# Causal attention and a gated MoE layer on one core: several 32-column blocks in one VectorE transpose, the 1e-9 added on ScalarE or GpSimd, and a table of offsets for the planner's due times

## The chip, the core and the metric

The kernel runs on one core of a Trainium2 chip. The metric is the device time of one execution in microseconds (us), the median of several runs.

The engines are named as the profile names them: PE is TensorE (PEld its weight loads), DVE is VectorE, ACT is ScalarE, POOL is GpSimd, and SP is SyncE, which here issues nearly all DMAs.

## The reference

```python
# q, k, v: (4, 12, 448, 64); w_gate, w_val: (768, 1536); w_out: (1536, 768), all float32
scores = scale * np.matmul(q, k.transpose(0, 1, 3, 2))
mask = np.triu(np.ones((seq, seq), dtype=bool), k=1)
scores = np.where(mask, -1000000000.0, scores)
scores = scores - np.max(scores, axis=-1, keepdims=True)
attn = np.exp(scores)
attn = attn / (np.sum(attn, axis=-1, keepdims=True) + 1e-09)
attn_out = np.matmul(attn, v).astype(np.float32)
x = np.ascontiguousarray(attn_out.transpose(0, 2, 1, 3)).reshape(B * S, H * D)   # (1792, 768)
g = x @ w_gate
silu = g * (1.0 / (1.0 + np.exp(-g)))
out = (silu * (x @ w_val) @ w_out).astype(np.float32)
```

## The kernel before, in words

**Chunks and units.** The work is cut into four chunks, one for each batch element (448 tokens). The attention of a chunk has 12 heads, numbered as units: units 0 to 11 are chunk 0, 12 to 23 chunk 1, 24 to 35 chunk 2, 36 to 47 chunk 3. Two heads make a pair that shares its loads. While the MoE products of one chunk run on PE, the attention of the next chunk is computed beside them. In the names of tiles the first number is the unit or the chunk: `S46_0_0` holds scores of unit 46, `M2_4` is the fifth gate or value product of chunk 2 (even numbers gate, odd ones value), `MO1_3` the fourth block of outputs of chunk 1. Chunks 2 and 3 share their products in a Strassen-like scheme (`early`, `pair`, `outputs`; tiles `Bb` and `Be`).

**Precision.** PE multiplies float32 as three products of a high and a low part (`xh`, `xl`, and the two halves of `whl`), lines 1063 to 1065. So each weight tile of 128x768 has to be split before PE can use it: a copy for the high part (L338, L341, L344), a subtraction for the low part (L360 on DVE, L363 on POOL). PSUM has two banks for the products, tag `M`, and `whl` has four buffers.

**One unit of attention** (`attention`, L437). Scores on PE (L555); the mask and the row maximum in one DVE instruction with a small read of the accumulator behind it (L606); the exponential on ACT with the row sums as a by-product (L618); the reciprocal of the sums on DVE (`recip`, L626); the division, on ACT, POOL or DVE (L663, L667, L671); a transposition; and the product with V (`weigh`). The sums of a unit lie in a tile of 128x4, one column for each block of rows.

**The 1e-9.** `recip` adds it by a reduction over two slots of `all_sums`, that of the unit and one that holds 1e-9, and takes the reciprocal of the result:

```python
sm, rc = all_sums[:, u % NR :: NR - u % NR, i0:i1], rec[u % NR][:, i0:i1]
nc.vector.tensor_reduce(rc, sm.rearrange("p a c -> p c a"), mybir.AxisListType.X, ALU.add)
nc.vector.reciprocal(rc, rc)
```

**The transposition.** For chunk 0 and five of the six pairs of chunk 1, PE transposes 128x128 blocks into PSUM (L730, L735, L770). For one pair of chunk 1 and all of chunks 2 and 3 it goes another way (`turn`, L789): DVE transposes 32x32 blocks within SBUF (L818), DMAs write the result to DRAM in another order (L838 to L841) and read it back. Each DVE instruction handles 128 columns of one block of rows. An even unit takes 1, 2 and 3 of them for its row blocks 1 to 3, an odd one 1, 2, 3 and 4 for its row blocks 0 to 3:

```python
for t in range(i, 2 * i + 1) if odd else range(i):
    ...
    nc.vector.transpose(s["stage"][:r, :, at : at + G],
                        s[f"pp{i}"][:r, P * t : P * t + P].rearrange("p (c n) -> p c n", c=4))
```

**The order of the work.** Nothing is scheduled on the chip. While the program is built, a planner (`Planner.run`, L109) keeps a modelled clock for each engine and picks, of the operations that could start next on an engine, the one with the earliest due time; where several engines can do an operation it also picks the engine. Due times come from constants: `LEN` and `ATT` say where a stage lies, `SLOPE`, `BOOST`, `WLEAD` and others how far an operation is due ahead of its use. What comes out is one fixed list for each engine, and each engine works its list strictly in order: an instruction that waits holds up everything behind it on that engine.

**What the gate does** (`activate`, L1091). When a gate product is done, ACT takes its tanh (L1097) and DVE multiplies it in (L1100); only then is its bank of PSUM free for a later product. When the value product is done, DVE multiplies again (`finish_h`, L1114).

## Time and profile before

| | |
|---|---|
| median of 3 runs | 642.06 us (640.26 to 642.89) |
| the profiled execution | 640.58 us, its span 638.8 us |
| PE busy | 624.3 us, 98% of the span, 3590 matmuls |
| DVE busy | 528.3 us, 83%, 1289 instructions |
| ACT busy | 406.0 us, 64%, 966 instructions |
| POOL busy | 247.2 us, 39%, 293 instructions |
| mean granted clock of PE | 0.997 of full speed |

The span runs from the first to the last instruction, and 1.8 us of the time lie around it. The ends of matmuls are modelled, and one begins before the last has ended, so a busy PE says that matmuls were under way, and not that they followed each other at their fastest; idle time of PE is certain. A wait is put down to the releaser that came last by the profile.

### The profile page before, as it was taken

The page shows a single profiled execution, that of the slowest core. Times are in us where ns is not written, and L with a number is a line of the kernel's source. Part 1 is how long each engine was busy: PE and PEld are TensorE (multiplying, and loading weights), DVE is VectorE, ACT ScalarE, POOL GpSimd, SP SyncE. Part 2 cuts the span into 40 slices and gives each one's busy share as a digit, 9 for nine tenths or more (in the row PEclk, how much of TensorE's full clock was granted, in tenths as well). Part 3 has the DMA queues.
Part 4 walks back from the last instruction along what each step waited for, and adds up shares of the span by engine and source line. Part 5 has one row for each costly group of instructions (what it writes and reads, how often), then busy time and mean ns, then how long its engine had stood idle before and what let it go on. Part 6 is the DMA issues. An engine that isn't in the chain of part 4 may idle for free.

```text
span 638.8 us, 11236 instructions
## 1 busy us (share of the span) xinstructions
PE 624.3 (98%) x3590; PEld 561.7 (88%) x3590; DVE 528.3 (83%) x1289; ACT 406.0 (64%) x966; POOL 247.2 (39%) x293
## 2 busy tenths in 40 slices
PE   9999999999999999999999988799999999999997
PEld 6569989899999999999999977699999999999997
DVE  6989889898899788979799999889998889895320
ACT  6999668597785557657768987865554444471100
POOL 3754623355263345444434555442024244440000
PEclk9999999999999999999999999899999999999999
DMA  8869987998877668683878678787353331156311
GB/s 279 292 221 309 285 301 263 351 330 297 290 283 227 238 184 268 202 257 96 264 237 261 204 213 265 234 294 243 117 160 128 127 105 62 77 168 196 107 44 43
DMA packets 72668, 136.08 MB, mean 213 GB/s; under 512 B 18081, under 2 KB 45473, under 8 KB 72609
## 3 DMA queue, kind: packets, MB, share of 16 engines
q1 hardware_dynamic: 72304, 135.04, 64.5%
q8 instruction: 28, 0.46, 0.3%
q10 hardware_dynamic: 304, 0.33, 0.2%
q14 instruction: 32, 0.25, 0.1%
HBM read 98.34 MB, written 37.00 MB: 212 GB/s over the span
## 4 chain that ended last, share of the span: by engine, by line
PE 83%; DVE 8%; DMA 4%; ACT 3%; issue 1%; SPq 0%; ACTq 0%; DVEq 0%
PE M L1063 10%; PE M L1064 9%; PE M L1065 9%; PE MO L1063 8%; PE MO L1064 8%; PE MO L1065 8%; PE S L555 5%; PE O L932 4%; PE Bb L1375 3%; PE Bb L1377 3%; PE Bb L1376 3%; PE T L770 2%; DMA wide<-in_w_dram 2%; PE Be L1375 2%; PE Be L1376 2%; PE Be L1377 2%
## 5 line engine op out<-in xcount | busy, mean ns | idle before, releaser
L1063 PE MATMUL M<-xh,whl 128*128 128x448 f32 x360 | 134.2, 373 | 6.8 <-DVE t(2, 2, 't')_5663 L1100 3.6
L1065 PE MATMUL M<-xh,whl 128*128 128x448 f32 x360 | 131.0, 364 | 0.9 <-DVE whl L360 0.9
L1064 PE MATMUL M<-xl,whl 128*128 128x448 f32 x360 | 130.9, 364 | 0.0
L360 DVE TENSOR_TENSOR whl<-wraw,whl 128x768 fp32r<-128x768 f32 x89 | 89.4, 1013 | 12.7 <-ACT whl L338 12.2
L618 ACT ACTIVATE p<-p,m 128x192 f32<-128x192 f32 (+3 forms) x180 | 91.2, 509 | 6.8 <-DVE m L606 6.3
L338 ACT ACTIVATE whl<-wraw 128x768 fp32r<-128x768 f32 x65 | 54.5, 840 | 40.8 <-PE MO L1065 23.5
L1063 PEld LDWEIGHTS M<-xh,whl 128*128 128x128 f32 x360 | 67.9, 189 | 13.4 <-DVE t(2, 2, 't')_5663 L1100 3.9
L606 DVE CUSTOM_DVE_ANT_0 p<-S,masks 128x192 f32<-128x192 f32 (+3 forms) x180 | 69.1, 426 | 8.2 <-PE S L555 7.9
L1065 PEld LDWEIGHTS M<-xh,whl 128*128 128x128 f32 x360 | 67.9, 189 | 6.1 <-DVE whl L360 1.3
L1064 PEld LDWEIGHTS M<-xl,whl 128*128 128x128 f32 x360 | 68.0, 189 | 3.8
L1063 PE MATMUL MO<-h,whl 128*128 128x448 f32 x162 | 59.4, 367 | 0.0
L1064 PE MATMUL MO<-h,whl 128*128 128x448 f32 x162 | 58.7, 362 | 0.0
L1065 PE MATMUL MO<-h,whl 128*128 128x448 f32 x162 | 58.5, 361 | 0.0
L663 ACT ACTIVATE p<-p,rec 128x320 f32<-128x320 f32 (+3 forms) x123 | 52.5, 482 | 4.5 <-DVE rec L631 4.1
L818 DVE STREAM_TRANSPOSE w<-p 128x128 f32<-128x128 f32 x192 | 40.6, 272 | 0.5 <-ACT p L663 0.2
L1049 DVE SCALAR_TENSOR_TENSOR wraw<-wide,top 128x768 uint32<-128x768 uint32 x36 | 35.9, 996 | 5.8 <-ACT top L338 4.7
L555 PEld LDWEIGHTS S<-KS,QS 64*128 64x128 f32 (+1 forms) x432 | 29.5, 174 | 6.6 <-issue 4.6
L618 ACT ACTIVATION_READ_ACCUMULATOR p<-p,m 128x1 f32 (+1 forms) x180 | 34.0, 189 | 0.0
L1063 PE MATMUL MO<-last,whl 128*128 128x448 f32 x90 | 33.4, 371 | 0.0
L555 PE MATMUL S<-KS,QS 64*128 64x448 f32 (+3 forms) x432 | 32.5, 295 | 0.4 <-POOL KS L363 0.4
L1064 PE MATMUL MO<-last,whl 128*128 128x448 f32 x90 | 32.6, 362 | 0.0
L1065 PE MATMUL MO<-last,whl 128*128 128x448 f32 x90 | 32.5, 361 | 0.0
(380 smaller groups left out, 1518.1 us busy)
## 6 DMA issues: line engine op xcount, KB each, us to landing
wide<-in_w_dram SPq DMA_DIRECT2D x36, 768.0 KB, 7.2
wraw<-wr SPq DMA_DIRECT2D x66, 384.0 KB, 4.3
wr<-wraw SPq DMA_DIRECT2D x36, 384.0 KB, 4.2
wr<-wr SPq DMA_DIRECT2D x24, 384.0 KB, 4.2
x<-dO SPq DMA_DIRECT2D x12, 608.0 KB, 6.1
vraw<-in_v_dram SPq DMA_DIRECT2D x24, 256.0 KB, 3.9
qraw<-in_q_dram SPq DMA_DIRECT2D x23, 224.0 KB, 4.9
kraw<-in_k_dram SPq DMA_DIRECT2D x23, 224.0 KB, 5.4
```

The lines of the kernel that those rows point to most:

```text
L338: nc.scalar.activation(out(), in_(), AF.Copy, scale=scale)
L360: r["DVE"] = (cost("DVE", "two", n), lambda: nc.vector.tensor_tensor(out(), a(), b(), alu))
L555: nc.tensor.matmul(st[u + y][f"S{i}"][:r], Q[:, q0 : q0 + r], K[:, :q1_] if y else K[:, S - q1_ :], start=z == 0, stop=z == len(passes) - 1)
L606: nc.vector.tensor_tensor_reduce(p[:r], s[f"S{i}"][:r], mask[:r, maskX - q0 : maskX - q0 + q1_] if h % 2 else back[:r, P - min(q1_, P) : P ...
L618: nc.scalar.activation(p[:r], p[:r], AF.Exp, bias=peak(i)[:r], scale=-1.0, accum_out=sums[u % NR][:r, i : i + 1],)
L663: nc.scalar.activation(p[:r], p[:r], AF.Copy, scale=rec[u % NR][:r, i : i + 1])
L818: nc.vector.transpose(s["stage"][:r, :, at : at + G], s[f"pp{i}"][:r, P * t : P * t + P].rearrange("p (c n) -> p c n", c=4))
L1049: nc.vector.scalar_tensor_tensor(w["raw"].bitcast(U32), z, 13, top, ALU.logical_shift_right, ALU.bitwise_or)
L1063: nc.tensor.matmul(out[:, :n], a[:, w], xhi, start=first, stop=False, skip_group_check=True)
L1064: nc.tensor.matmul(out[:, :n], a[:, w], xlo, start=False, stop=False, skip_group_check=True)
L1065: nc.tensor.matmul(out[:, :n], l[:, w], xhi, start=False, stop=bool(last), skip_group_check=True)
L1375: nc.tensor.matmul(ps[key][:, :T], sh, hi, start=first, stop=False, skip_group_check=True)
```

## The change

Three things are changed together.

1. `turn` looks for runs of 128-column blocks whose places in the staging tile are evenly spaced, and transposes such a run by one DVE instruction with a four-dimensional access pattern. So that runs occur, the even units keep their two groups of blocks in the other order in the staging tile, and the readers (`view`, `groups`) take them from there. The planner's price of it goes from 0.06 us and 128 columns for each block to 128 columns for each block and 0.138 us for each instruction.
2. The reduction leaves `recip`. The 1e-9 is added to the unit's sums in place, either by ACT or by POOL, as the planner chooses; `recip` then waits for this addition.
3. The planner's constants are others, and every due time gets an offset from a table, `SHIFT`, by the name of the function that made the operation and its numbers. The table has 332 entries, from -96.43 to 58.75.

```diff
-SLOPE0 = 1.25
-WLEAD = 1.54
-XD = [-10.0, 3.0]
+SLOPE0 = 1.515
+WLEAD = 1.415
+XD = [6.364, 2.157]
...
-LEN = [47.162, 116.0, 276.388, 93.293, 128.599, 80.135]
-ATT = [(0.0, 1.421), (42.885, 110.356), (162.6, 245.2), (420.604, 89.521)]
-FRAC0 = 0.675
-SLOPE = 1.24
-BOOST = 5.8
+LEN = [57.293, 137.864, 266.214, 76.452, 83.944, 91.479]
+ATT = [(20.774, 25.636), (52.817, 111.405), (163.387, 233.644), (414.797, 104.249)]
+FRAC0 = 0.846
+SLOPE = 3.154
+BOOST = 14.007
...
-VLEADS = {0: 7.849, 1: 18.0, 2: 37.244, 3: 48.013}
+VLEADS = {0: -2.04, 1: 35.488, 2: 49.344, 3: 43.827}
...
+SHIFT = {
+    "": 0.77, "attention0": -24.87, "attention1": -21.61, "attention10": 3.28, "attention11": 4.59, "attention12": 0.29, "attention13": -0.26,
...
     def op(alts, due, deps=(), alloc=(), uses=(), extra=0.0):
+        due += SHIFT.get(label[0], 0.0)
...
-            sm, rc = all_sums[:, u % NR :: NR - u % NR, i0:i1], rec[u % NR][:, i0:i1]
-            nc.vector.tensor_reduce(rc, sm.rearrange("p a c -> p c a"), mybir.AxisListType.X, ALU.add)
-            nc.vector.reciprocal(rc, rc)
-        rc = op({"DVE": (0.3, recip)}, due(5), exps, [], [rsum])
+            nc.vector.reciprocal(rec[u % NR][:, i0:i1], sums[u % NR][:, i0:i1])
+
+        def plus():
+            i0, i1 = U.own[0][0], U.own[-1][0] + 1
+            sm = sums[u % NR][:, i0:i1]
+            nc.scalar.activation(sm, sm, AF.Identity, bias=all_sums[:, NR, 0:1])
+
+        def plus_pool():
+            i0, i1 = U.own[0][0], U.own[-1][0] + 1
+            sm = sums[u % NR][:, i0:i1]
+            nc.gpsimd.tensor_scalar(sm, sm, 1.0e-9, None, ALU.add)
+        ad = op({"ACT": (0.2, plus), "POOL": (0.2, plus_pool)}, due(4.5), exps, [], [rsum])
+        rc = op({"DVE": (0.18, recip)}, due(5), [ad], [], [rsum])
...
-                for t in range(i, 2 * i + 1) if odd else range(i):
+
+                def spot(t):
                     j = t - i if odd else i - t
-                    at = n3 * odd + n3 * (j >= 2) + G * place(i, j) if j else (3 * n3 if i == 0 else G * (i - 1))
-                    nc.vector.transpose(s["stage"][:r, :, at : at + G],
-                                        s[f"pp{i}"][:r, P * t : P * t + P].rearrange("p (c n) -> p c n", c=4))
+                    return (n3 + n3 * (j >= 2) if odd else n3 * (j < 2)) + G * place(i, j) if j else (3 * n3 if i == 0 else G * (i - 1))
+                t, end = (i, 2 * i + 1) if odd else (0, i)
+                while t < end:
+                    n, a0 = 1, spot(t)
+                    step = spot(t + 1) - a0 if t + 1 < end else G
+                    while step > 0 and t + n < end and spot(t + n) == a0 + n * step:
+                        n += 1
+                    src = s[f"pp{i}"][:r, P * t : P * (t + n)].rearrange("p (t c n) -> p t c n", t=n, c=4)
+                    to = s["stage"][:r, :, a0 : a0 + (n - 1) * step + G].rearrange("p c (s n) -> p s c n", n=G)[:, :: max(step // G, 1)]
+                    nc.vector.transpose(to, src)
+                    t += n
...
-            o = op({"DVE": (k * (0.06 + P / 960), blockwise)}, due(6.2), deps + tps[:1], rS if new else [], [rps[i]] + ([] if new else rS))
+            m = (1, 1, 2, 2)[i] if odd else (0, 1, 1, 2)[i]
+            o = op({"DVE": (k * P / 960 + m * 0.138, blockwise)}, due(6.2), deps + tps[:1], rS if new else [], [rps[i]] + ([] if new else rS))
```

How this moves instructions is seen at three places of the lists. Lines of the changed kernel have other numbers: L606 becomes L669, L618 L681, L818 L900, L1100 L1188, L1063 to L1065 L1150 to L1152, and the addition on ACT is L697.

**DVE, ahead of the gate of the third gate product of chunk 2** (`t(2, 2)`, fed by `M2_4`). Before, the last rows in front of it are these, `w45` being the staging tile of unit 45 and `p44` the weights of its pair:

```order
L818 STREAM_TRANSPOSE w44_5644<-p44_3_5335 128x4x32 x3
L818 STREAM_TRANSPOSE w45_5679<-p44_0_5300 64x4x32
L818 STREAM_TRANSPOSE w45_5679<-p44_1_5306 128x4x32 x2
L818 STREAM_TRANSPOSE w45_5679<-p44_2_5320 128x4x32 x3
L818 STREAM_TRANSPOSE w45_5679<-p44_3_5335 128x4x32 x4
L630 TENSOR_REDUCE rec_70<-sums_69 128x4
L631 RECIPROCAL rec_70<-rec_70 128x4
L606 ISA p46_3_5580,m47_5608<-S47_0_0_5491,masks_67 128x448
L606 ISA m47_5608 128x1
L1100 SCALAR_TENSOR_TENSOR t(2, 2, 't')_5663<-t(2, 2, 't')_5663,M2_4_5543 128x448
```

In the changed kernel the same transpositions of unit 45 stand here:

```order
L1203 TENSOR_TENSOR t(2, 1, 't')_5524<-t(2, 1, 't')_5524,M2_3_5475 128x448
L900 STREAM_TRANSPOSE w45_5563<-p44_0_5212 64x4x32
L900 STREAM_TRANSPOSE w45_5563<-p44_1_5215 128x2x4x32
L900 STREAM_TRANSPOSE w45_5563<-p44_2_5218 128x2x4x32
L900 STREAM_TRANSPOSE w45_5563<-p44_2_5218 128x4x32
L900 STREAM_TRANSPOSE w45_5563<-p44_3_5224 128x2x4x32 x2
L692 RECIPROCAL rec_70<-sums_69 128x4
```

Ten instructions have become six, the reduction is gone, and twelve rows of later work stand between these and the gate of `M2_4`. Ahead of that gate DVE's list had 1045 instructions and has 934; ahead of the end of `M2_4` PE's list has 2351 matmuls in both, of the same kinds.

**PE, where the scores of the last pair stand** (units 46 and 47). Before they stood in the middle of `M2_3`:

```order
L1065 MATMUL M2_2_5383<-xh5_82,whl74_5161 128x448
L1063 MATMUL M2_3_5433<-xh3_80,whl75_5178 128x448
L1064 MATMUL M2_3_5433<-xl3_86,whl75_5178 128x448
L1065 MATMUL M2_3_5433<-xh3_80,whl75_5178 128x448
L555 MATMUL S46_0_0_5490<-KS46_5232,QS46_5230 128x448
```

Now they stand near the start of `M2_1`:

```order
L1152 MATMUL M2_0_5276<-xh2_79,whl72_5072 128x448
L1150 MATMUL M2_1_5301<-xh0_77,whl73_5158 128x448
L1151 MATMUL M2_1_5301<-xl0_83,whl73_5158 128x448
L1152 MATMUL M2_1_5301<-xh0_77,whl73_5158 128x448
L618 MATMUL S46_0_0_5308<-KS46_5210,QS46_5201 128x448
```

They have moved ahead from matmul 2280 to matmul 2226. The scores of other pairs moved further: those of unit 26 from 1229 to 1048, of unit 28 from 1363 to 1195, of unit 36 from 1902 to 1764, of unit 40 from 2036 to 1976.

**ACT, in chunk 0**, at the third unit's sums. Before:

```order
L618 ACTIVATE p2_3_314,sums_69<-p2_3_314,m3_322 128x448
L585 ACTIVATE p4_0_369,sums_69<-p4_0_369,m4_370 128x64
L618 ACTIVATE p4_1_382,sums_69<-p4_1_382,m4_370 128x192
L663 ACTIVATE p2_2_307<-p2_2_307,rec_70 128x320
L618 ACTIVATE p4_2_387,sums_69<-p4_2_387,m4_370 128x320
```

In the changed kernel:

```order
L681 ACTIVATE p2_3_292,sums_69<-p2_3_292,m3_312 128x448
L648 ACTIVATE p4_0_374,sums_69<-p4_0_374,m4_375 128x64
L697 ACTIVATE sums_69<-sums_69 128x3
L400 ACTIVATE ph2_1_401<-T2_1_389 128x384
L681 ACTIVATE p4_3_377,sums_69<-p4_3_377,m4_375 128x448
```

The addition stands between an exponential and a copy out of PSUM. Of the 48 additions, 27 are on ACT and 21 on POOL. Up to the last exponential of chunk 0 ACT's list had 79 instructions and has 89.

## Rows read from the trace of the kernel before

**Rows 1.** The page's first part: busy time and its share of the span.

```profile
span 638.8 us, 11236 instructions
PE 624.3 (98%) x3590; PEld 561.7 (88%) x3590; DVE 528.3 (83%) x1289; ACT 406.0 (64%) x966; POOL 247.2 (39%) x293
```

**Rows 2.** Stretches: start and end, length, busy time by engine, clock, DMA.

```profile
0.00:16.00 16.00, 14.42 (x102) 9.62 (x102) 10.03 (x47) 10.92 (x36) 5.85 (x16) 1.00 0.81 279
16.00:47.00 31.00, 31.00 (x241) 18.86 (x237) 27.92 (x98) 30.18 (x93) 20.75 (x29) 1.00 0.77 263
47.00:163.00 116.00, 114.76 (x690) 104.74 (x689) 105.17 (x242) 88.94 (x209) 51.49 (x57) 1.00 0.87 301
163.00:200.00 37.00, 37.00 (x231) 34.17 (x230) 33.77 (x93) 28.60 (x71) 16.62 (x19) 1.00 0.80 280
200.00:360.00 160.00, 160.00 (x956) 148.29 (x955) 139.15 (x410) 110.23 (x282) 70.22 (x88) 1.00 0.72 226
360.00:420.00 60.00, 51.93 (x306) 46.13 (x303) 55.58 (x172) 48.04 (x127) 29.46 (x35) 0.97 0.73 217
420.00:580.00 160.00, 160.00 (x806) 148.56 (x805) 144.48 (x217) 83.28 (x146) 52.85 (x49) 1.00 0.45 147
```

**Rows 3.** Waits of PE: line, releaser, us in total, times, longest.

```profile
PE M L1063 <- DVE t(2, 2, 't')_5663 L1100: 3.6, 1, 3.6
PE M L1063 <- ACT s L1199: 2.2, 2, 1.2
PE O L932 <- DVE ph L360: 1.2, 2, 1.0
PE M L1063 <- DVE t(0, 4, 't')_1438 L1100: 1.0, 1, 1.0
```

**Rows 4.** Timeline of PE around its longest wait: start, us, instruction, idle before.

```profile
406.94 0.37 PE L1065 MATMUL M<-xh,whl 128*128 128x448 f32 x1
410.86 0.74 PE L1063 MATMUL M<-xh,whl 128*128 128x448 f32 x1 [3.55 <-DVE t(2, 2, 't')_5663 L1100]
...
413.64 0.53 PE L1064 MATMUL M<-xl,whl 128*128 128x448 f32 x1
414.01 0.36 PE L1065 MATMUL M<-xh,whl 128*128 128x448 f32 x1
```

**Rows 5.** The stretch behind that wait, in the columns of rows 2.

```profile
410.80:414.00 3.20, 3.14 (x8) 2.81 (x9) 2.97 (x8) 2.59 (x6) 0.69 (x2) 0.50 0.48 108
```

**Rows 6.** Timeline of DVE during that wait.

```profile
406.88 2.61 DVE L818 STREAM_TRANSPOSE w<-p 128x128 f32<-128x128 f32 x13
409.42 0.12 DVE L630 TENSOR_REDUCE rec<-sums 128x4 f32<-128x8 f32 x1
409.57 0.18 DVE L631 RECIPROCAL rec<-rec 128x4 f32<-128x4 f32 x1
...
410.19 0.62 DVE L1100 SCALAR_TENSOR_TENSOR t(2, 2, 't')_5663<-t(2, 2, 't')_5663,M 128x448 f32<-128x448 f32 x1
```

**Rows 7.** Groups by form: busy us, mean ns of one, idle before.

```profile
L818 DVE STREAM_TRANSPOSE w<-p 128x128 f32<-128x128 f32 x180 | 38.0, 271 | 0.5 <-ACT p L663 0.2
L606 DVE CUSTOM_DVE_ANT_0 p<-S,masks 128x448 f32<-128x448 f32 x48 | 29.2, 612 | 0.5 <-PE S L555 0.4
L606 DVE CUSTOM_DVE_ANT_0 p<-S,masks 128x192 f32<-128x192 f32 x48 | 16.6, 347 | 0.1
L671 DVE TENSOR_SCALAR p<-p,rec 128x448 f32<-128x448 f32 x16 | 7.4, 460 | 0.1
```

**Rows 8.** Groups of ACT and POOL by form, in the same columns.

```profile
L618 ACT ACTIVATE p<-p,m 128x448 f32<-128x448 f32 x48 | 31.6, 659 | 1.6 <-DVE m L606 1.3 <-DVE rec L630 0.3
L618 ACT ACTIVATE p<-p,m 64x64 f32<-64x64 f32 x36 | 12.2, 338 | 3.8 <-DVE m L606 3.7
L338 ACT ACTIVATE osb<-MO 128x448 f32<-128x448 f32 x15 | 8.1, 543 | 37.1 <-PE MO L1065 37.0
L667 POOL TENSOR_SCALAR p<-p,rec 64x64 f32<-64x64 f32 x3 | 1.4, 465 | 2.5 <-DVE top L341 2.1 <-DVE rec L631 0.4
```

More of the change, by code (lines that the diff above doesn't have):

```diff
@@ L52 @@
 VIA = {1: [1], 2: range(6), 3: range(6)}
-VLEADS = {0: 7.849, 1: 18.0, 2: 37.244, 3: 48.013}
+VLEADS = {0: -2.04, 1: 35.488, 2: 49.344, 3: 43.827}
 HOP = 2.2
+SHIFT = {
[49 rows of a table added]
+}
 FEW = 72
@@ L323, with named, run @@
     heads = {}
+    label = [""]
+    def named(f):
+        def run(*a, **k):
+            was, label[0] = label[0], f.__name__ + "_".join(str(x) for x in a if isinstance(x, int))
+            r = f(*a, **k)
+            label[0] = was
+            return r
+        return run
     def op(alts, due, deps=(), alloc=(), uses=(), extra=0.0):
+        due += SHIFT.get(label[0], 0.0)
         first = [heads[r.tag] for r in alloc if r.tag in heads]
@@ L435, in later_keys @@
         return o[:, :, G * (j - 1) :], p[:, :, : 3 * G - G * (j - 1)] if j < 3 else p[:, :, 2 * G :]
+    @named
     def attention(u):
@@ L787, in attention @@
             weigh(u)
+    @named
     def turn(u, s, U, due, norms, rps):
@@ L857, in turn @@
             lv, rv = loads[u, "v"]
-            view = lambda k: lambda: s["turned"][:, row : row + 8 * n3].rearrange("p (b n) -> p b n", b=4)[:, :, n3 * (k - 1) : n3 * k]
+            at_ = lambda k: n3 * (k - 1 if odd else 2 - k)
+            view = lambda k: lambda: s["turned"][:, row : row + 8 * n3].rearrange("p (b n) -> p b n", b=4)[:, :, at_(k) : at_(k) + n3]
             for j in range(1, 4):
@@ L901, in turn @@
         for g in (1, 2):
-            pair(g, groups(g - 1), rP, 0, P, 4 * n3, rd)
+            pair(g, groups(g - 1 if odd else 2 - g), rP, 0, P, 4 * n3, rd)
+    @named
     def weigh(u):
@@ L988 @@
     xsplit = {}
+    @named
     def split_x(c, k):
@@ L1012, in fetch_weights @@
         return op({"SP": (0.3, load), "kb": 384}, due, [stored[g]], [rw]), rw
+    @named
     def weights(i, due=None):
@@ L1068 @@
     m3 = 3 * cost("PE", "r", T)
+    @named
     def gate_up(c, f, w, bankof, at, hold=None):
@@ L1109, in halves @@
         return a, l, alloc[0], alloc[1]
+    @named
     def finish_h(c, key, f, due, t2, rt, last, rM):
@@ L1116, in finish_h @@
         return t3
+    @named
     def project(c, m, fs, at, wi, h_ops, where, key, tag, first=True, last=True):
@@ L1297 @@
     where = {}
+    @named
     def pair(n):
```

48 rows, old and new, of the table SHIFT are left out of this document.

## The prediction

> **What bounds the kernel now.** I read the page's busy times first, then the stretches, then PE's waits, and then the timeline of PE and DVE around the longest of them. PE is busy for 98% of the span [rows 1]; of 638.8 us it idles 14.5. The stretches say where [rows 2]: 1.58 us up to 16, nothing from 16 to 47, 1.24 from 47 to 163, nothing from 163 to 360, then 60 - 51.93 = 8.07 from 360 to 420, and nothing again until 580. What is left, some 3.5 us, is the end, where the last result is copied and stored. So apart from start and end there is one bad stretch, and in it DVE is 55.58 of 60 us busy, while in the 160 us ahead of it DVE idles 160 - 139.15 = 20.85.
>
> The largest of PE's waits is there: 3.6 us for the gate of `t(2, 2)` on DVE; two waits of 2.2 in total are for copies by ACT, and others for low parts that DVE makes [rows 3]. The timeline shows what a late DVE does: PE starts its last matmul at 406.94 and the next at 410.86 [rows 4]. In this time DVE works through 13 transpositions, a reduction, a reciprocal and a row maximum, which stand ahead of the gate in its list, and reaches the gate at 410.19 [rows 6]. Behind the wait PE's clock is granted at 0.50, the lower of its two levels, 1.2 GHz [rows 5]: eight matmuls take from 410.86 to 414.01, 3.15 us, where at 2.4 GHz one starts every 0.20 us, as from 414.01 on. That costs another 3.15 - 1.6 = 1.55 us. The engine had idled 3.55 us before the clock fell.
>
> **The change part by part.** PE's own list keeps all its instructions: 3474 rows before and after. What can be won is therefore idle time and clock: 8.07 + 1.55 in the bad stretch, 1.24 between 47 and 163, little more.
>
> The reductions. All 48 go. From the start of one to the start of the reciprocal behind it are 409.57 - 409.42 = 0.15 us [rows 6]; DVE is spared 7.2 us. The addition that takes its place comes to 27 on ACT and 21 on POOL. No row of ACT has four columns. Exponentials of 448 and of 64 columns take 659 and 338 ns [rows 8], 0.836 ns a column; carried on to 4 columns that is 0.29 us, which I take; the ends are 0.10, if it hides behind its neighbours, and the 0.34 of the 64-column row. On POOL the nearest row is 0.465 [rows 8]; POOL is busy 39% and the addition costs it nothing that PE would see, as long as the transposition of the same unit stands many instructions behind, which it does. If that cover fails, the reciprocal is late by about 0.5 us and then the divisions behind it.
>
> The transpositions. There are 208 blocks, one instruction each; now 78 instructions take two blocks and 52 one. Thirteen in a row go from 406.88 to 409.42, 0.195 each [rows 6]. Row maxima of 448 and 192 columns differ by 265 ns [rows 7], 1.035 ns a column, so the 128 columns of a block are 0.132 and what an instruction adds at this pace is 0.063. Two blocks in one instruction I put at 2 x 0.132 + 0.063 = 0.33 in place of 0.39. The ends: no gain at all, if the four-dimensional pattern costs what it saves, and 0.139 spared (the 271 ns of the row [rows 7] less 0.132), if the whole fixed part of a row is spared. I take the pace, since DVE's list is full there and pace is what counts. That is 78 x 0.063 = 4.9 us, bounds 0 and 10.8.
>
> The new order. This is the greater part. Ahead of the gate of `M2_4`, the one that PE waited for, PE has done the same 2351 matmuls before and after, but DVE has 934 instructions ahead of it and not 1045. Of the 111 that are gone, 47 are reductions (47 x 0.15 = 7.05 us) and 72 are saved by joining blocks (72 x 0.063 = 4.5); so 8 others have been added in the balance, and they are divisions of 448 columns, 8 x 0.46 = 3.7 [rows 7]. DVE reaches this gate with 7.05 + 4.5 - 3.7 = 7.9 us less behind it, against a wait of 3.55. Even with no gain from joining it is 3.4, nearly the wait itself. And the 13 transpositions no longer stand directly ahead of it. Since the scores of the pairs moved ahead too (the last from matmul 2280 to 2226, others by 60 to 180 matmuls), the 8.07 us should go: the copies and low parts that PE waited for there are late because they queue on the same full DVE. I take 8.07 and the clock's 1.55.
>
> What moved ahead has to fit where it lands. Ahead of the gate of `M1_0` DVE's list has 510 instructions in place of 506, although 26 reductions (3.9 us) have left it: 11 more row maxima (mean of the two rows 0.48, 5.3 us), 8 more divisions (3.7) and 16 more blocks transposed, by 30 instructions in place of 32 (16 x 0.132 = 2.1). That is 7.2 us by these durations, and as rows overlap, some 6 us more work at a place to which PE comes after 1268 matmuls, not 1256. DVE idles 37 - 33.77 = 3.23 us in the stretch from 163 to 200 and 20.85 in the next [rows 2], and that is the cover. I charge nothing; if this cover is gone, the bound is 6 us.
>
> The start. From 16 to 47 ACT is busy 30.18 of 31 us, PE without a gap [rows 2]. Up to the last exponential of chunk 0 ACT's list grows from 79 to 89 instructions: four additions (1.2 us) and six others, at some 0.48 (between the 0.338 and 0.659 of rows 8), 2.9. Of these 4.1 us, 0.8 fit into ACT's idle time, and 9 more matmuls of the first products stand ahead of the transpositions of the last unit of chunk 0, 9 x 0.20 = 1.8 of work for PE. I charge 4.1 - 0.8 - 1.8 = 1.5, ends 0 and 4.1.
>
> The stretch from 47 to 163. Its largest wait, 1.0, is for the gate `t(0, 4)` [rows 3], ahead of which DVE's list has 224 instructions, not 251. I take the 1.0.
>
> The sum against the profiled execution: 640.58 - 8.07 - 1.55 - 1.0 + 1.5 = 631.5. That execution lies 1.5 below the median of the three runs, 642.06, at the lower end of their range; for the median of the changed kernel I add 1.0 and forecast **632.5**.
>
> **The rivals.**
>
> *Two products in turns.* In the new PE list two products often alternate, three matmuls each, on the two banks: at eight places, among them `MO1_1` with `MO1_2` and `M1_22` with `M1_23`. `MO1_2` ends six matmuls after `MO1_1`, and `MO1_3` follows at once, so 6 x 0.20 = 1.2 us must do for a copy out of the bank of 0.543 [rows 8], its hand-over and whatever stands ahead of it. Before, a whole product of 36 matmuls, 7.2 us, lay between. Against it: ACT and DVE share these copies. The nearest wait is the longest one for ACT's copies, 1.2 [rows 3]. If half of the eight places cost that, the time is 632.5 + 4.8 = 637.3.
>
> *ACT bounds the start.* If none of its 4.1 us is hidden, the time is 632.5 + 2.6 = 635.1. For it speaks how full ACT is there, against it that PE has the first products to fill in with. The Trainium skill (ScalarE: Activation LUTs, Rules for kernel authors) speaks against this part of the change: an addition belongs on VectorE and not on ScalarE, and an ACTIVATE with a pointer as its bias has a fixed part of about 280 ns. By that figure four additions would be 1.1 us, an estimate, where the rows give 1.2; no run here has yet shown one.
>
> *The joined transposition does not do what it says.* If two blocks cost as much as two instructions or more, DVE's relief at the bad gate falls to 3.4 us or below, and the stretch from 360 to 420 stays as full as it was, apart from the order. Half of the 9.6 us or less would be won: 637 to 642, say 640.
>
> *The work lands where DVE is full: slower.* From 163 to 200 DVE is 33.77 of 37 us busy already. If its 3.23 us of idle time are waits for others and can't be used, the 6 us of work ahead of the gate of `M1_0` reach PE as a wait, with a fall of the clock behind it (1.55), and if the waits from 360 to 420 come from the order and not from DVE's load, they stay. That is 642.06 + 6 + 1.55 = 649.6. It decides from the point at which PE idles over 3 us between 163 and 230. For it speaks that one late gate made a wait of 3.6 us; against it that DVE idles most just behind this stretch.
>
> **How the numbers follow.** My forecast has 0.55, two products in turns 0.18, ACT at the start 0.08, the joined transposition 0.07, the slower case 0.12. About 0.5% (3.2 us) is what a measurement of this kernel can tell from no change: faster means below 638.9, slower above 645.3. Faster is the forecast, the ACT case and three quarters of the bank case, 0.55 + 0.08 + 0.14 = 0.77; the same is the rest of the bank case and the transposition, 0.11; slower 0.12. The range begins at 627: all the idle time and clock outside start and end, 8.07 + 1.55 + 1.24, off the profiled execution gives 629.7, and 2.7 less if the start also loses its 1.58 us and ACT's charge turns into a gain of 1. It ends at 641 and takes in the bank case and most of the transposition's; out of it lie the slower case and the tails, not over 0.2.
>
> **What would show it.** In the changed profile: no TENSOR_REDUCE, 130 transpositions, of which those of two blocks start 0.33 us apart; DVE some 10 us less busy; PE idle under 2 us from 360 to 420 and its clock at 1.00 in every stretch; ACT's additions at 0.29; PE idle 1 to 2 us from 16 to 50. The forecast is wrong if PE's waits name gates or copies of chunk 1 between 163 and 230, if they name copies out of the banks behind products that take turns, or if the clock falls in some other stretch.

## The result and the profile after

| | before | after |
|---|---|---|
| median | 642.06 us (640.26 to 642.89) | **632.45 us** (632.20 to 633.67), five runs |
| ratio | | 0.9855, 95% interval 0.9837 to 0.9874 |
| the profiled execution, its span | 640.58, 638.8 us | 632.45, 630.7 us |

The forecast was 632.5, between 627 and 641. The page's first part for the changed kernel stands against [rows 1]:

```profile
span 630.7 us, 11116 instructions
PE 623.1 (99%) x3590; PEld 561.2 (89%) x3590; DVE 517.0 (82%) x1168; ACT 416.9 (66%) x1001; POOL 251.3 (40%) x301
```

DVE is busy for 11.3 us less, ACT for 10.9 and POOL for 4.1 more. PE's work is the same; it idles 7.6 us of its span in place of 14.5. The stretches, in the columns of [rows 2], say where:

```profile
0.00:16.00 16.00, 13.55 (x85) 9.05 (x86) 8.90 (x39) 9.99 (x32) 5.38 (x17) 1.00 0.83 284
16.00:47.00 31.00, 31.00 (x238) 18.20 (x237) 29.45 (x96) 30.93 (x102) 19.37 (x27) 1.00 0.84 291
47.00:163.00 116.00, 115.62 (x717) 105.21 (x716) 106.56 (x232) 88.64 (x217) 52.00 (x62) 1.00 0.84 290
163.00:200.00 37.00, 37.00 (x232) 33.96 (x231) 34.44 (x93) 32.28 (x86) 19.52 (x22) 1.00 0.84 284
200.00:360.00 160.00, 160.00 (x957) 148.58 (x956) 141.82 (x365) 118.96 (x302) 79.33 (x96) 1.00 0.75 236
360.00:420.00 60.00, 59.03 (x331) 52.80 (x329) 52.68 (x139) 50.57 (x126) 26.86 (x35) 1.00 0.82 250
420.00:580.00 160.00, 159.90 (x809) 149.68 (x808) 133.91 (x198) 79.52 (x136) 48.89 (x46) 1.00 0.43 138
```

From 360 to 420 PE idles 0.97 us and not 8.07, its clock is granted in full in every stretch shown, and DVE, which had 20.85 us of idle time from 200 to 360, now works 2.67 us more there although its instructions are cheaper. Against that stands the start: up to 16 PE idles 2.45 us, not 1.58. PE's waits, as in [rows 3], have a new first row:

```profile
PE T L842 <- ACT p L735: 1.2, 1, 1.2
PE warm L356 <- DVE xs L351: 1.0, 1, 1.0
PE M L1150 <- ACT s L1289: 0.7, 3, 0.4
PE T L807 <- POOL p L739: 0.4, 1, 0.4
```

What the new instructions cost is in the groups by form (busy us, mean ns of one, idle before; [rows 7, 8] for before):

```profile
L900 DVE STREAM_TRANSPOSE w<-p 128x256 f32<-128x256 f32 x72 | 27.3, 401 | 0.0
L900 DVE STREAM_TRANSPOSE w<-p 128x128 f32<-128x128 f32 x36 | 10.0, 279 | 0.5 <-ACT p L735 0.3
L692 DVE RECIPROCAL rec<-sums 128x4 f32<-128x4 f32 x42 | 6.8, 165 | 1.9 <-ACT sums L697 0.8 <-POOL sums L702 0.7
L702 POOL TENSOR_SCALAR sums<-sums 128x4 f32<-128x4 f32 x19 | 6.7, 354 | 18.2 <-ACT p L681 11.8 <-DVE KS L422 2.6 <-ACT p L735 1.9
L697 ACT ACTIVATE sums<-sums 128x4 f32<-128x4 f32 x23 | 6.7, 292 | 0.3
```

A row's mean is its whole length, and rows overlap. The pace shows on a timeline of DVE, where one row holds five transpositions, one of one block and four of two, nine blocks in 1.60 us:

```profile
380.27 1.60 DVE L900 STREAM_TRANSPOSE w<-p 128x256 f32<-128x256 f32 x5
```

From start to start a two-block one takes 0.326 us and a single one some 0.194, in the median of those that follow each other directly.

**Gain and loss along the way.** PE does the same matmuls in another order. At places where both kernels have done the same set, the changed one is 1.9 us late at the end of the first scores, 3.2 late at 71 us, 1.1 late at 142, then 3.9 early at 400, 8.5 early at 417, 7.5 at 421 and 8.1 early at PE's last matmul. Of the 1.9, 0.9 was there before PE waited for anything that the change had moved: the eight warm-up products (`warm`) took 1.04 us in this execution and 0.62 before, and the scores behind them longer too.

### The profile page after: what moved, and what is told of

Its sections match the earlier page's. It is cut to its first block, busy times and chain, and to the rows that moved or that the text cites. A ratio compares the mean times of both kernels' runs of the same rounds, so it can differ in the third digit from the quotient of the medians.

```text
span 630.7 us, 11116 instructions
## 1 busy us (share of the span) xinstructions
PE 623.1 (99%) x3590; PEld 561.2 (89%) x3590; DVE 517.0 (82%) x1168; ACT 416.9 (66%) x1001; POOL 251.3 (40%) x301
## 4 chain that ended last, share of the span: by engine, by line
PE 83%; DVE 6%; DMA 5%; ACT 4%; issue 1%; POOL 0%; ACTq 0%; SPq 0%; DVEq 0%; POOLq 0%
PE M L1150 10%; PE M L1151 10%; PE M L1152 10%; PE MO L1150 9%; PE MO L1151 9%; PE MO L1152 9%; PE S L618 7%; PE O L1017 5%; DMA wr<-wr 3%; PE T L842 2%; PE O L1062 2%; PE Bb L1467 2%; PE Bb L1466 2%; PE Bb L1468 2%; PE Be L1468 1%
## 5 line engine op out<-in xcount | busy, mean ns | idle before, releaser
L1150 PE MATMUL M<-xh,whl 128*128 128x448 f32 x360 | 133.7, 371 | 0.9 <-ACT s L1289 0.7
L1152 PE MATMUL M<-xh,whl 128*128 128x448 f32 x360 | 130.4, 362 | 0.0
L422 DVE TENSOR_TENSOR whl<-wraw,whl 128x768 fp32r<-128x768 f32 x86 | 83.9, 983 | 21.1 <-ACT whl L400 20.7
L681 ACT ACTIVATE p<-p,m 128x192 f32<-128x192 f32 (+3 forms) x180 | 91.1, 509 | 2.3 <-DVE m L669 2.0
L400 ACT ACTIVATE whl<-wraw 128x768 fp32r<-128x768 f32 x72 | 60.2, 840 | 34.1 <-PE MO L1152 19.8
L1150 PEld LDWEIGHTS M<-xh,whl 128*128 128x128 f32 x360 | 67.5, 188 | 7.8 <-ACT s L1289 2.8
L1152 PEld LDWEIGHTS M<-xh,whl 128*128 128x128 f32 x360 | 67.5, 187 | 4.7
L669 DVE CUSTOM_DVE_ANT_0 p<-S,masks 128x192 f32<-128x192 f32 (+3 forms) x180 | 68.3, 424 | 3.5 <-PE S L618 3.3
L1150 PE MATMUL MO<-h,whl 128*128 128x448 f32 x162 | 59.7, 369 | 0.0
L1152 PE MATMUL MO<-h,whl 128*128 128x448 f32 x162 | 58.5, 361 | 0.0
L735 ACT ACTIVATE p<-p,rec 128x192 f32<-128x192 f32 (+3 forms) x128 | 53.9, 478 | 4.6 <-DVE rec L692 4.5
L900 DVE STREAM_TRANSPOSE w<-p 128x256 f32<-128x256 f32 (+2 forms) x120 | 36.3, 354 | 0.6 <-ACT p L735 0.3
L618 PEld LDWEIGHTS S<-KS,QS 64*128 64x128 f32 (+1 forms) x432 | 29.6, 174 | 6.3 <-issue 4.1
L681 ACT ACTIVATION_READ_ACCUMULATOR p<-p,m 128x1 f32 (+1 forms) x180 | 34.1, 190 | 0.0
L425 POOL TENSOR_TENSOR whl<-wraw,whl 128x768 fp32r<-128x768 f32 x16 | 29.5, 1848 | 9.2 <-DVE whl L422 3.1
L1150 PE MATMUL MO<-last,whl 128*128 128x448 f32 x90 | 33.1, 368 | 0.0
L1152 PE MATMUL MO<-last,whl 128*128 128x448 f32 x90 | 32.6, 362 | 0.0
```

Source lines behind the costliest of these rows:

```text
L400: nc.scalar.activation(out(), in_(), AF.Copy, scale=scale)
L422: r["DVE"] = (cost("DVE", "two", n), lambda: nc.vector.tensor_tensor(out(), a(), b(), alu))
L618: nc.tensor.matmul(st[u + y][f"S{i}"][:r], Q[:, q0 : q0 + r], K[:, :q1_] if y else K[:, S - q1_ :], start=z == 0, stop=z == len(passes) - 1)
L669: nc.vector.tensor_tensor_reduce(p[:r], s[f"S{i}"][:r], mask[:r, maskX - q0 : maskX - q0 + q1_] if h % 2 else back[:r, P - min(q1_, P) : P ...
L681: nc.scalar.activation(p[:r], p[:r], AF.Exp, bias=peak(i)[:r], scale=-1.0, accum_out=sums[u % NR][:r, i : i + 1],)
L735: nc.scalar.activation(p[:r], p[:r], AF.Copy, scale=rec[u % NR][:r, i : i + 1])
```

## The experiments

Two ideas stood against each other: that the gain is the new order (which work stands where in DVE's list), or that it is the cheaper DVE instructions. Mine was a sum of both. The new plan also gives some instructions to other engines: leaving the reductions, the transpositions, the reciprocals and the additions aside, DVE has 990 instructions in place of 985, ACT 974 in place of 966, POOL 280 in place of 293. What is called the order below includes this; no run takes it apart. In all versions below that keep a list, the order of every other instruction is the same, so the same matmul can be compared by its start.

### The order and the cheaper instructions, taken apart

**The new order with the old instructions** (`e3_both`): one block per transposition, and the reduction back in `recip` with the addition gone from ACT and POOL.

```diff
-                    while step > 0 and t + n < end and spot(t + n) == a0 + n * step:
-                        n += 1
...
-            nc.vector.reciprocal(rec[u % NR][:, i0:i1], sums[u % NR][:, i0:i1])
+            nc.vector.tensor_reduce(rc, sm.rearrange("p a c -> p c a"), mybir.AxisListType.X, ALU.add)
+            nc.vector.reciprocal(rc, rc)
...
-            nc.scalar.activation(sm, sm, AF.Identity, bias=all_sums[:, NR, 0:1])
+            return
...
-            nc.gpsimd.tensor_scalar(sm, sm, 1.0e-9, None, ALU.add)
+            return
```

> The new order alone: the changed kernel's lists with one block per transposition and with the old reductions, so that every instruction costs what it did before; DVE has about 12 us more work than in the changed kernel. My theory: the order still spreads the load better, but DVE comes to the gates of 360 to 420 without reserve: 639 us, PE idle 5 us or more from 360 to 420. Rival A (cheaper instructions do it all): as before the change or worse, 642 or more. Rival B (the order does it all): 632.5, within 1.

Measured: 634.82 us (633.88 to 636.48), ratio 0.9893 (0.9871 to 0.9916); the kernel before, measured beside it, 642.27. So 7.45 of the 9.6 us come with every instruction at its old price. My 639 was wrong, and so was "within 1": the rest, 2.4 (634.82 less 632.45), is the cheaper instructions'. Three stretches of this version up to 420:

```profile
163.00:200.00 37.00, 37.00 (x231) 34.11 (x230) 34.44 (x103) 31.62 (x84) 18.60 (x19) 1.00 0.83 284
200.00:360.00 160.00, 160.00 (x957) 148.60 (x956) 144.71 (x427) 117.26 (x293) 78.20 (x90) 1.00 0.74 235
360.00:420.00 60.00, 57.70 (x324) 51.58 (x323) 53.42 (x163) 49.35 (x121) 26.60 (x33) 1.00 0.82 243
```

DVE is busy 144.71 us from 200 to 360, before it was 139.15 [rows 2]: 5.6 us of work at the old prices now lie in time in which DVE had idled. Up to 360 it has done 9.8 us more than before (325.8, not 316.0), and as the plan also leaves it 4.5 us less in all (523.8, not 528.3), it goes on from there with 14.3 us less to come. PE's 2.30 us of idle time from 360 to 420 name no gate; 2.1 of them are for ACT's copies `s` out of the banks. The longest is this one, ahead of which ACT had waited 0.95 us for a reciprocal of DVE and then 0.92 for a store:

```profile
413.40 0.47 PE L1150 MATMUL M<-xh,whl 128*128 128x448 f32 x1 [1.49 <-ACT s L1289]
```

**One block per transposition in the new order** (`e1_single`, the first part of the diff above alone).

> The changed kernel, in its own order, but with one block of weights per transposition (208 instructions in place of 130). DVE has 78 x 0.063 = 4.9 us more work, no engine's list changes otherwise. My theory (new order and less DVE work share the gain; DVE comes to the gates of 360 to 420 with too little lead without the joined blocks): the reserve at the gate falls from 7.9 to 3.4 us, against the wait of 3.55, so about half of the 9.6 us come back: 637 us, PE idle some 4 us from 360 to 420. Rival A (cheaper instructions do it all): of about 12 us that DVE was spared 4.9 are taken back, 9.6 x 4.9 / 12 = 3.9: 636.4. Rival B (the order does it all): 632.5, within 0.7, PE idle from 360 to 420 as in the changed kernel, about 1 us.

Measured: 631.29 us (630.60 to 632.47), ratio 0.9839 (0.9814 to 0.9864). Not slower at all, and PE idles 0.44 us from 360 to 420:

```profile
360.00:420.00 60.00, 59.56 (x340) 54.31 (x338) 54.45 (x160) 51.79 (x127) 27.52 (x35) 1.00 0.82 252
```

My theory and rival A both fall here.

**The reduction back, transpositions joined** (`e2_reduce`, the other parts of that diff).

> The changed kernel, in its own order, with the old reduction back in front of each reciprocal on DVE; ACT and GpSimd add nothing. DVE has 48 x 0.15 = 7.2 us more, ACT 23 x 0.29 = 6.7 us less, GpSimd 21 to 25 small operations less. My theory: 47 of the 48 stand ahead of the gates of 360 to 420, so the reserve there falls from 7.9 to 0.9 us, below the wait of 3.55: most of the gain of that stretch goes, less what the start wins by not waiting for the addition (0.5 us): 638 us. Rival A (cheaper instructions do it all): 9.6 x 7.2 / 12 = 5.8 lost: 638.3. Rival B (the order does it all): 632.5 or up to 0.5 less, since the reciprocal of the first unit no longer waits for GpSimd. Rival C (ACT's additions cost 1.5 to 2 us in chunk 0): the progress of PE at 47 us is 1.5 us ahead of the changed kernel's.

Measured: 633.89 us (632.78 to 634.30), ratio 0.9874 (0.9852 to 0.9896): 1.4 us lost by the medians, with ranges that overlap, and nothing like 5.5. The wait at the start is not from the addition either. PE waits 1.23 us for the same division with the reduction on DVE, as it does in the changed kernel:

```profile
11.63 0.30 PE L844 MATMUL T<-ident,p 128*128 128x128 f32 x1 [1.23 <-ACT p L737]
```

So rival C falls: at 47 us this version is only 0.8 us ahead of the changed kernel, and it was 0.7 ahead already when the second pair's scores began.

**The old order with the cheaper instructions** (`e5_old_cheap`): the kernel before with joined transpositions, and with `recip` cut to the reciprocal of the plain sums.

> The cheaper instructions alone: the kernel before, its lists unchanged in order, with joined transpositions and with the 1e-9 left out (the reciprocal reads the plain sums, no addition anywhere), so that DVE has 12 us less work and no engine has more. This kernel leaves out the addition of 1e-9. My theory: DVE reaches the gate of the longest wait 11 us of work earlier, if it can use that time: the waits on DVE from 360 to 420 fall, but DVE idles already ahead of that stretch, so that only what is saved inside the full stretch counts, about 13 transpositions and what stands near them, some 3 us; the wait of 3.55 and the half clock behind it shrink, those for ACT's copies (2.2) stay: 637 us. Rival A (cheaper instructions do it all): 632.5. Rival B (the order does it all): 641 to 642.

Measured: 640.46 us (637.31 to 643.06, twelve runs), ratio 0.9977 (0.9956 to 0.9997). Rival B's 641 to 642 is nearest, my 637 was wrong. The long wait for the gate of `t(2, 2)` is 3.06 us in place of 3.55, and the clock still falls behind it:

```profile
200.00:360.00 160.00, 160.00 (x965) 148.30 (x963) 136.98 (x354) 110.94 (x285) 70.34 (x89) 1.00 0.71 225
360.00:420.00 60.00, 52.86 (x295) 46.97 (x296) 55.39 (x148) 48.28 (x125) 29.58 (x36) 0.97 0.76 227
```

DVE's saving went into its idle time ahead of 360 (136.98 busy, before 139.15); from 360 to 420 DVE is as full as it was. Cheaper instructions in the old order bring 1.8 us, in the new one 2.4, and the order brings 7.5 with dear ones and 8.0 with cheap ones.

### Is it what stands directly ahead of the gate?

**One instruction moved** (`e10_gate`): the kernel before, with the gate of `t(2, 2)` right behind its tanh in the program, ahead of the 13 transpositions.

```diff
+        if key == (2, 2, "t"):
+            early_ops.append(o)
...
+    for o in early_ops:
+        order.remove(o)
+        order.insert(order.index(o.deps[0]) + 1, o)
```

> The kernel before with one instruction moved: on DVE the gate of t(2, 2), for which PE waited 3.55 us, stands ahead of the 13 transpositions and the low part before them, right where its input from ACT is ready (406.82); nothing is cheaper, every other instruction keeps its place. Theory of the order (rival B, which the runs so far favour: what counts is what stands directly ahead of an instruction that PE waits for): PE goes on 3.2 us earlier and the clock does not fall, 3.2 + 1.55 = 4.7 us: 637.4. My theory of the load (DVE is full from 360 to 420, so work pushed behind the gate makes the next wait): the transpositions come 0.6 us later, at most 1 us of the wait is gone after the next products: 641.

Measured: 642.18 us (641.32 to 643.86, twelve runs), ratio 1.0004 (0.9991 to 1.0017): nothing. PE's timeline shows why. The wait is down to 0.22, the clock holds, PE is 4.6 us ahead, and nine matmuls later it waits 3.54 us for what stood behind the gate:

```profile
407.72 0.47 PE L1064 MATMUL M<-xh,whl 128*128 128x448 f32 x1 [0.22 <-DVE t(2, 2, 't')_5663 L1101]
...
409.43 0.36 PE L1066 MATMUL M<-xh,whl 128*128 128x448 f32 x1
413.33 0.62 PE L933 MATMUL O<-ph,VS 128*128 128x448 f32 x3 [3.54 <-DVE ph L360]
```

```profile
408.05 2.61 DVE L819 STREAM_TRANSPOSE w<-p 128x128 f32<-128x128 f32 x13
...
412.56 1.27 DVE L360 TENSOR_TENSOR ph<-x,ph 64x448 fp32r<-64x448 f32 x2 [0.59 <-ACT ph L338]
```

The second fence is DVE, and between its rows lies this one of ACT:

```profile
411.01 0.35 ACT L664 ACTIVATE p<-p,rec 64x64 f32<-64x64 f32 x1 [2.53 <-DVE rec L632]
```

The transpositions came 1.2 us later, and with them the reciprocal behind them; ACT waited 2.53 us for it, since a division stands ahead of its copies, and only after a copy could DVE make the low part (`ph`) that the product with V needs. Within a stretch in which DVE is 55 of 60 us busy, moving one instruction only renames the wait. Behind the new wait the clock falls too (0.97 over the stretch, as before the change). So "the order" is not what stands directly ahead of one gate. That it is how much DVE work is still to come when the stretch begins is my reading; the ledger below is for it, and the leads below (`e14_lead`) do not fit it.

### The start

**The first reciprocals earlier** (`e8_start`): the changed kernel, with the reciprocals of units 0 and 1 and the divisions behind them moved ahead of the next pair's row maxima and exponentials.

```diff
+        if u < 2:
+            early_ops.extend([ad, rc, *norms.values()])
...
+    k = 0
+    for o in sorted(early_ops, key=lambda o: order.index(o)):
+        order.remove(o)
+        k = max([k - 1] + [order.index(d) for d in o.deps]) + 1
+        order.insert(k, o)
+        k += 1
```

> The changed kernel with the reciprocals of the first two units, and the divisions behind them, ahead of the next pair's row maxima (DVE) and exponentials (ACT). If the wait of 1.23 us for the first transposition comes from that order, the reciprocal starts near 10.05 and not 11.45, and PE's wait falls to 0.3 or less: 631.4. If it comes from the addition that stands between exponential and reciprocal now, or if the time is given back behind it (the small wait at 48.6, a full ACT from 16 to 47): 632.4.

Measured: 632.11 us (631.73 to 632.65), ratio 0.9844 (0.9828 to 0.9860). The cause of the wait is right. In the changed kernel DVE idles for the next scores and the reciprocal follows two row maxima, although POOL had the sums ready at 9.95 (rows of POOL and DVE, then the row of PE's timeline):

```profile
9.73 0.22 POOL L702 TENSOR_SCALAR sums<-sums 128x4 f32<-128x4 f32 x1 [6.36 <-ACT p L681]
```

```profile
10.75 0.22 DVE L643 CUSTOM_DVE_ANT_0 p<-S,both 128x64 f32<-128x64 f32 x1 [1.44 <-PE S L618]
...
11.45 0.17 DVE L692 RECIPROCAL rec<-sums 128x4 f32<-128x4 f32 x1
```

```profile
12.81 0.30 PE L842 MATMUL T<-ident,p 128*128 128x128 f32 x1 [1.23 <-ACT p L735]
```

Moved, the wait of 1.23 is gone and PE runs 1.7 us ahead from 21 to 400. But little of that is the move's. PE's inputs came sooner in that execution: it was 2.0 us ahead just before the place of the wait, 3.3 just behind it, and 1.7 at 21. Other waits had come in its place, the longest this one for POOL's division:

```profile
10.55 0.76 PE L845 MATMUL T<-ident,p 128*128 128x128 f32 x5 [0.72 <-POOL p L740]
```

The same move shows the same in the version with single blocks below, against `e1_single`, where the inputs came alike: nothing ahead of the wait, 1.2 us behind it, 0.2 from 20 on. So most of what the move wins is given back within ten microseconds. At 412 the rest of the lead is gone as well. PE's list stands at 401 behind ACT's copy `s` out of a bank, and that copy waits for the store of an earlier `s`, whose buffer it takes; here the row of ACT in the changed kernel and in this one:

```profile
400.89 0.54 ACT L1289 ACTIVATE s<-M 128x448 f32<-128x448 f32 x1 [2.50 <-DMA ks<-s]
```

```profile
400.19 0.54 ACT L1292 ACTIVATE s<-M 128x448 f32<-128x448 f32 x1 [3.53 <-DMA ks<-s]
```

The store was issued 1.74 us earlier (391.70, not 393.44), but landed only 0.7 earlier. In this version, what PE was ahead at 400 ends there and at the next such wait, at 411.54.

**Both** (`e11_both`): this and one block per transposition.

> The changed kernel with both: one block per transposition and the earlier reciprocals of the first two units. If the 1.2 us that the single blocks were below the changed kernel are real and the start is kept: 630.2. If they were the spread between runs: as the start alone, 631.4. If neither is kept: 632.4.

Measured: 632.59 us (631.70 to 633.42), ratio 0.9851 (0.9833 to 0.9869). So the 1.2 us by which the single blocks lay below the change were not kept. Joining was worth 0.9 with the reductions in place (634.82 to 633.89), minus 1.2 without them (631.29 to 632.45), and 0.5 with the earlier start (632.59 to 632.11): together nothing that these runs can tell. In the single-block version the copy at this place waited for PE and not for the store:

```profile
399.11 0.55 ACT L1287 ACTIVATE s<-M 128x448 f32<-128x448 f32 x1 [1.25 <-PE M L1150]
```

From 388 to 402 its three stores of `s` landed after 2.9 us at the median, those of the changed kernel after 4.4 (the groups of DMA issues, KB each and median us to landing; the changed kernel, then the single blocks):

```profile
ks<-s SPq DMA_DIRECT2D x3, 224.0 KB, 4.4
```

```profile
ks<-s SPq DMA_DIRECT2D x3, 224.0 KB, 2.9
```

The store that the copy waited for took some 7.4 us in the change, issued at 393.44. Joining isn't what slows it: with the single blocks and the earlier start (`e11_both`) the copy waits 2.41 us for it too. Why it landed sooner in one version is open, and that the store makes the difference is read from these rows; a version with a third buffer was not tried.

### Where the order comes from

**No shifts** (`e6_noshift`): the changed kernel with `SHIFT = {}`.

> The changed kernel with the new planner constants but the table of shifts empty: new prices, cheaper instructions, an order that the planner makes from the constants alone. If the constants (attention planned earlier and spread over a longer time) bring the order's gain: 633 to 636, PE idle from 360 to 420 under 3 us. If the shifts, fitted operation by operation, bring it: 640 or more, with waits of 1 us and more on single copies and gates.

Measured: 630.39 us (629.96 to 630.89), ratio 0.9817 (0.9801 to 0.9833). The table of 332 shifts brings nothing; without it the kernel is 2.1 us faster. There the longest wait of PE from 360 to 420 is 0.32 us.

**The constants alone, in the kernel before** (`e12_const`): the nine lines from `SLOPE0` to `VLEADS` of the change, nothing else.

> The kernel before with only the nine lines of planner constants exchanged for the new ones: old instructions, old prices, no addition on ACT or GpSimd, one block per transposition, no shifts. If the gain is the new order, and the constants make that order: 633 to 636, as the new order with old instructions (634.8). If the cheaper instructions have to be in the planner's prices for it: 638 or more.

Measured: 640.96 us (638.55 to 643.69, twelve runs), ratio 0.9980 (0.9963 to 0.9998). The constants alone do not make the gain. The new plan with the same old instructions, 634.82, was made with the additions and the new prices in the planner as well as the shifts, and as the shifts bring nothing, I put it to the prices; no run has them with the constants and nothing else.

**The new prices with the old constants** (`e7_oldconst`): those nine lines set back, and no shifts.

> The changed kernel with the old planner constants and no shifts: joined transpositions, additions on ACT and GpSimd, new prices, order planned by the old constants. If the constants make the gain: 639 to 642, with PE idle 5 us or more from 360 to 420, as with the cheaper instructions in the old order (640.5). If a new plan with the new prices alone would do: under 636.

Measured: 649.51 us (648.50 to 654.82), ratio 1.0132 (1.0096 to 1.0167), slower than before and outside both forecasts. The planner has put the low part of one weight tile on POOL, where it starts late, after an idle time of 1.50 us put down to DVE, and PE waits 6.7 us (PE's waits):

```profile
PE M L1102 <- POOL whl L375: 6.7, 1, 6.7
PE M L1102 <- DVE whl L372: 3.6, 2, 3.3
```

**The leads set back** (`e14_lead`): no shifts, `SLOPE = 1.24`, `BOOST = 5.8`, the rest of the constants new.

> The changed kernel without shifts, and of the new constants the lead of gates and copies and the spread of a unit's stages set back (BOOST 14.007 to 5.8, SLOPE 3.154 to 1.24); the lengths of the stretches, the attention's times and its leads stay new. If it is the attention's earlier work that counts (DVE's load moved into its idle time ahead of 360): 630 to 633. If it is the lead of gates and copies over the transpositions (what stands ahead of an instruction that PE waits for): 637 or more, with waits on gates again.

Measured: 637.99 us (637.13 to 640.05), ratio 0.9936 (0.9912 to 0.9961). Setting these leads back costs 7.6 us, the outcome foretold for the second idea, though PE's longest waits in the bad stretch are on low parts by DVE, 1.5 for `ph` and 1.2 for `whl`, and not on gates (PE's waits):

```profile
PE M L1102 <- DVE whl L372: 2.0, 3, 1.2
PE O L967 <- DVE ph L372: 1.5, 1, 1.5
```

So early DVE work isn't all that the new order brings: it also takes how far gates, copies and the stages of a unit are due ahead of the rest. The constants without the prices, the prices without the constants, and the plan without these leads each lose most or all of the gain, or over half of it; only the shifts can go.

**The faster version** (`e13_best`): no shifts, and the earlier reciprocals of `e8_start`.

> The version without shifts (630.4) with the reciprocals of the first two units ahead of the next pair's row maxima and exponentials. There PE waits 1.24 us for the first transposition, and from 360 to 420 no longer than 0.3 for anything, so that, unlike in the changed kernel, nothing late in the kernel should take the start's gain back: 629.2. If it is taken back there too: 630.4.

Measured: **629.83 us** (629.60 to 630.16), ratio 0.9806 (0.9780 to 0.9832), 2.6 below the change. The wait at the start is gone; what is left of PE's waits is small:

```profile
PE warm L306 <- DVE xs L301: 1.0, 1, 1.0
PE O L970 <- POOL ph L375: 0.3, 1, 0.3
PE O L1015 <- ACT ph L350: 0.2, 1, 0.2
PE M L1103 <- ACT s L1242: 0.2, 1, 0.2
```

Against 630.39 the 0.6 lies about at the spread between runs, and is half of the 1.2 forecast. By PE's starts the move wins 1.3 us here, of which 0.6 are left at 21.

**A ledger.** DVE's busy time still to come at 360 us (its whole busy time less that of the stretches up to 360) sorts the versions, roughly. At that point each has begun between 2203 and 2229 of its 3590 matmuls.

| version | DVE left at 360 | time |
|---|---|---|
| before | 212.3 us | 642.06 |
| gate moved | 212.1 | 642.18 |
| old order, cheaper | 210.1 | 640.46 |
| new prices, old constants | 207.6 | 649.51 |
| new constants alone | 199.8 | 640.96 |
| leads set back | 198.9 | 637.99 |
| the change, reduction back | 198.4 | 633.89 |
| new order, old instructions | 197.9 | 634.82 |
| the change, single blocks and earlier start | 196.1 | 632.59 |
| the change | 195.9 | 632.45 |
| the change, single blocks | 195.8 | 631.29 |
| the change, earlier start | 193.4 | 632.11 |
| no shifts | 186.8 | 630.39 |
| no shifts, earlier start | 187.4 | 629.83 |

It isn't all, and it is a comparison of six plans and their variants, not a test: no run moves DVE work ahead of 360 and changes nothing else. Three plans have too little lead at single places (6.7 us for `whl`; two waits of over 1 us behind 460 with the new constants alone; the low parts with the leads set back) and are slower than their load.

## Why the prediction was right, and where not

**The bad stretch, 8.07 and 1.55: right.** From 142 us, where the changed kernel is 1.1 late, to 417, where it is 8.5 early, it wins 9.5 us, of which 8.5 are left at 421; 9.62 was charged. No half clock is left, and PE idles 0.97 us from 360 to 420.

**The reserve at the gate: the step that failed.** I counted the instructions ahead of the gate of `M2_4`, gave the 7.9 us of DVE work fewer there as what removes the wait, and said that without joining it would be 3.4, "nearly the wait itself". By that count the new order with the old instructions, 7.05 + 4.5 - 7.9 = 3.65 us *more* work ahead of the gate than before, should have kept its wait or lengthened it. PE idles 2.3 us there from 360 to 420, none of it for a gate. An instruction's count ahead of a gate is not delay: DVE idled 20.85 us from 200 to 360, and the work that landed there left PE without a gap. The moved instructions, which I had named but given no price, were the gain; the cheaper ones, which I had made the whole of the reserve, bring 2.4 of 9.6.

**The reductions and the joined blocks.** The prices were right: no reduction is left, the next transposition starts 0.326 us behind one of two blocks, for which I took 0.33, and the rows of all 208 blocks cover 39.4 us of DVE's time in place of 44.1, 4.7 less, for which I took 4.9. That DVE is 11.3 us less busy doesn't bear this out by itself: with the old instructions in the new order it is already 4.5 less, so that the cheaper ones account for 6.8 where I had 12.1; and two versions with the same instructions, the change and `e8_start`, differ by 2.0 in DVE's busy time. What they are worth in time was not: 1.4 to 3.5 us for the reductions in the new order, nothing that can be told for the blocks. The rival that gave 637 to 642 without the joining's gain is refuted by 631.29.

**The additions.** On ACT 292 ns, for which I took 0.29. The Trainium skill (ScalarE: Activation LUTs, What ACT_TABLE_LOAD costs) has a fixed part of about 280 ns for an ACTIVATE with a pointer as its bias, and this row agrees. The rule of the Trainium skill (ScalarE: Activation LUTs, Rules for kernel authors) that an addition belongs on VectorE would have gained nothing here: with the reduction back on DVE, and nothing added on ACT or POOL, the kernel is 1.4 us slower by the medians. On POOL 354 ns and not 465.

**The start, 1.5: the size was off and the cause was another.** PE is 1.9 us late at once and 3.2 by 71. I put it down to ACT's longer list; the runs show that 1.2 are a wait (0.26 before the change) because the first reciprocal stands behind the next pair's row maxima, with the addition or without, and 0.9 were there ahead of it. The idle time of 1 to 2 us from 16 to 50 that I had foretold is 0.38; how PE loses the further 1.3 by 71 is open. And the wait costs the end next to nothing: taken away, it gives 0.3 of its 1.2, as other waits behind it take most of it back by 21.

**The gate `t(0, 4)`, 1.0.** The wait is gone, but from 71 to 142 the changed kernel makes up 2.1 us, twice what I took. With the start the two come to +1.1 in place of +0.5.

**The moved work, charged nothing: right.** PE has no gap from 163 to 360.

**The other rivals.** Two products in turns: PE waits 0.7 us in three places for copies out of the banks, where I gave the rival 4.8. With the start moved, the same waits are 2.7 in four, but there ACT's copies had waited for stores (3.53 and 0.80 us), which is not the rival's reason. Slower: not this change, but its prices without its constants are just that, 649.51, through a late low part on POOL and not where I had put it.

So the sum came out within 0.1 us while one of its reasons was wrong, and that closeness is luck. Against the profiled execution it said 631.5, and that execution took 632.45; the 1.0 added for the median filled the gap, although here the profiled execution is the median. Nor do single waits add up as if they were independent: two of them, the one at the start and the one for the gate of `t(2, 2)`, were taken away singly and gave 0.3 and 0.

## What to carry to other kernels

Moving the one late instruction behind which a wait is shown need not help: where its engine was busy 55 of 60 us, the next wait took its place. There, look first at idle time of that engine ahead of the stretch, and at the work that it still has to do when the stretch begins, and not only at the count of instructions ahead of the gate; that this sorts plans only roughly, the ledger shows. Make the same list with the old instructions, and the old list with the new ones, before giving the gain to either. And try a fitted table of corrections against none.

## What was not expected of the hardware

The store of one 224 KB tile landed after 2.9 us at the median in one version and 4.4 in another over the same 14 us of the program, with the DMA engines 82% busy from 360 to 420; through a pair of buffers this held ACT for 2.4 to 3.5 us and then PE. An addition of up to 128x4 took POOL 0.22 to 0.24 us in 17 of 21 cases and 0.59 to 1.20 in the other four; what lengthened those isn't known.
